# Half of the decay exponentials replaced by products on GpSimd, with the cosine's bias an immediate and the first transform of u in pairs of row tiles

## The chip, the cores and the metric

One core of a Trainium2 chip runs the kernel. The metric is the device time of one execution in microseconds (us). Engines are named as in the profile: PE is TensorE, PEld its weight load, ACT is ScalarE, DVE is VectorE, POOL is GpSimd, SP is SyncE (it issues most DMAs).

## The reference

The input is u, 2048 x 448 (L x D). Two branches read it and are mixed by a gate.

```python
# branch a: a diagonal state space model (N = 256 complex modes per channel), as a convolution
dt = exp(log_dt)
A = -exp(log_A_real) + 1j * A_imag
P = exp((A * dt[:, None])[:, :, None] * arange(L))        # D x N x L
K = 2 * einsum("dn,dnl->dl", C * dt[:, None], P).real     # D x L
a = irfft(rfft(u.T, 2 * L) * rfft(K, 2 * L))[:, :L].T + u * D_skip
# branch b: attention of 16 heads in 4 segments of 512, with a memory carried along
for s in range(4):
    p = softmax(q_s @ k_s.T * scale + mask)
    o_s = g * (phi(q_s) @ M) / (phi(q_s) @ z + 1e-6) + (1 - g) * (p @ v_s)
    M, z = M + phi(k_s).T @ v_s, z + phi(k_s).sum(l)      # phi(t) = t + 1 or exp(t)
b = o @ wo
gate = sigmoid((u * gate_w).sum(-1))
out = gate * a + (1 - gate) * b
```

## The kernel before

The first half, to about 448 us, makes the convolution kernel K and, between, the projections of the attention; the second half transforms K and u, multiplies, transforms back and does the attention. The change is in the first half.

**Parameters.** prepare_params (L178) works out the decay rate la = exp(log_A_real) dt, the angles and the coefficients, split into three bf16 parts each (parts, L227) and sent through DRAM (SD, SP) to be read as matmul weights (tiles lh). The tile cab holds a factor by which EX is multiplied.

**Decays, angles, products, sums.** A lag l is 64 b + r. The kernel sum over the 256 modes is done as products of X (coarse lags 64 b, tile EX times cosine or sine) with Y (fine lags r, tile EY times cosine or sine). first_half (L312) goes over 28 J of 16 channels each; n = 2 J + c are 56 steps of 8 channels, and four n make a group g, 0 to 13.

- decays(g), L422: for each of the group's two J three calls of decay (L339): two matmuls (ps_arg<-ce,lh, one for each row half) and one Exp of 128x1024: EY(J,0), EY(J,1), then EX(J), which POOL multiplies by cab (scale, L353, one TENSOR_TENSOR of 128x1024, L359). Six exponentials a group.
- turns(n), L361: eight matmuls give the angle in turns. trig(n), L376: ACT makes sine, abs, and the cosine as the sine of pi/2 less that (bias tile bhp); the result is the tile cs, of which there are two buffers.
- product(n), L386: four DVE instructions: X (L393), Y (L397, L398 and L399). sums(n), L401: 32 small matmuls ps_k<-Y,X.

Exp and Sin lie in different tables of ACT, so each group has two table loads. The order on each engine is that of the program's code, with decays of a group behind the product of the group before.

**Feed.** What PE, ACT and DVE do between these steps is doled out by the class Feed (L465). Its steps come from two generators: project (L678: for each of four segments s the transposes of xin, the products with the value weights (values), and 8 units, each 12 matmuls with a weight tile w of 448 KB loaded from WD; units go in pairs, and "pe" behind a pair holds the generator until the next call of exps), and transform_u (L513: 32 tiles of a first transform of u, ps_m<-ut,s1u, evicted to gs and stored to GU). spend(us) runs steps until their own nominal costs use up the budget; a step with a negative cost ends a spend. exps, called ahead of each Exp in decay, lets a held pair go on. The budget is PLACE (L460) at the six places of decays and 1.7 at each n, times RATES for the group. What is left at the end is run by feed.rest.

**Split weights.** In project, weights() splits wq and wk into a high part (ACT) and a rest (POOL, L721), in two tiles wsp of their own, and stores them to WD (queue of SP, L1394). The units load w (L733, two buffers) from WD. hi and lo of a unit go to QD or KD (L767).

A matmul is recorded under L1370 (helper mm), a transpose under L1373, most ACT instructions under L1335 (act and copy). The tile ps_m stands for PSUM buffers that all these steps share.

## Time and profile before

| | |
|---|---|
| median of 3 runs | 873.04 us (870.07 to 874.4) |
| span of the profiled execution | 866.7 us |
| first half / second half | 448.1 / 418.6 us |
| busy PE, DVE, ACT, POOL | 753.7, 596.9, 539.2, 173.1 us |
| one group of four n, mean of the last twelve | 27.5 us |

The span is that of one execution taken by the profiler; the runs were timed apart, and their median is 6.3 us above it. A line of the grouped view reads: line, engine, operation, output<-inputs by the program's names, shapes, count, then busy time in us and mean ns of one, then the idle time ahead and what ended it. In the timeline the first two numbers are start and duration in us. In the windows view each engine has its busy time and, in brackets, its instructions; the last three columns are the granted clock of PE, the DMA share and GB/s.

### The profile page before, as it was taken

To read this page: it belongs to the slowest core of one execution; us is meant where nothing else is said; L and a number is where in the kernel's file an instruction comes from. 1 tells how busy PE (TensorE), PEld (TensorE's weight loads), DVE (VectorE), ACT (ScalarE), POOL (GpSimd) and SP (SyncE) were. 2 spreads that over 40 slices of the span, in tenths; PEclk is the share of its full clock that TensorE was granted. 3 is DMA by queue.
4 is the path that set the end of the run, shared out by engine and by line. 5 is a ranking of instruction groups with operands and counts; after the bars stand their busy time and mean duration, and the time that the engine had idled before them with its cause. 6 is when DMAs were issued, how large, how long until landed. Compare 5 with 4: busy or idle time off the path is not lost.

```text
span 866.7 us, 18996 instructions
## 1 busy us (share of the span) xinstructions
PE 753.7 (87%) x7575; PEld 410.3 (47%) x7597; DVE 596.9 (69%) x1160; ACT 539.2 (62%) x638; POOL 173.1 (20%) x217
## 2 busy tenths in 40 slices
PE   1687988998879988799979799999997998888997
PEld 1364655765547644476534444444443443343443
DVE  7988778777787777877648656656664747664564
ACT  4876989798997999979842255544453434431220
POOL 5224111001110011101100111222313124222110
PEclk9998999998999999999979689999999999878799
DMA  9347753334633255323569948557465545654873
GB/s 242 91 110 247 227 185 104 96 111 154 205 124 96 96 169 194 122 92 132 178 218 347 317 133 264 178 193 249 139 222 189 193 162 168 216 187 164 221 231 100
DMA packets 88290, 153.11 MB, mean 177 GB/s; under 512 B 20626, under 2 KB 57162, under 8 KB 88154
## 3 DMA queue, kind: packets, MB, share of 16 engines
q1 hardware_dynamic: 79130, 140.83, 50.2%
q10 hardware_dynamic: 7424, 9.18, 3.1%
q0 software_dynamic: 1648, 1.89, 0.7%
q8 instruction: 60, 0.98, 0.5%
q14 instruction: 28, 0.23, 0.1%
HBM read 90.87 MB, written 60.63 MB: 175 GB/s over the span
## 4 chain that ended last, share of the span: by engine, by line
PE 52%; ACT 16%; DVE 13%; issue 7%; DMA 7%; POOL 2%; SPq 1%; ACTq 0%; DVEq 0%; POOLq 0%
PE ps_a L1370 18%; PE ps_m L1370 16%; PE ps_pv L1370 7%; ACT cs L1335 7%; PE ps_arg L1370 4%; DVE jk L992 3%; PE ps_k L1370 3%; PE ps_m L1373 2%; ACT L1335 2%; DVE Y L397 2%; DMA WD<-wsp 1%; ACT EX L1335 1%; DMA dn<-pvs 1%; DVE Y L398 1%; DMA ident<-in_c_id 1%
## 5 line engine op out<-in xcount | busy, mean ns | idle before, releaser
L1023 ACT ACTIVATE PT<-ps_a 128x1024 f32<-128x1024 f32 (+1 forms) x96 | 84.5, 881 | 122.9 <-PE ps_a L1370 115.9
L992 DVE CUSTOM_DVE_ANT_0 jk<-ps_a,mk 128x512 f32<-128x512 f32 (+3 forms) x256 | 124.9, 488 | 49.6 <-PE ps_a L1370 42.3
L359 POOL TENSOR_TENSOR EX<-EX,cab 128x1024 f32<-128x1024 f32 x28 | 54.0, 1928 | 309.3 <-ACT EX L1335 286.3
L1335 ACT ACTIVATE cs<-ps_arg 128x1024 f32<-128x1024 f32 x111 | 107.3, 1021 | 2.7 <-DVE Y L398 2.4
L1370 PE MATMUL ps_a<-qu,ku 32*128 32x512 f32 (+3 forms) x768 | 92.9, 364 | 1.3 <-DVE mx L992 0.6
L1370 PE MATMUL ps_m<-xh,w 112*128 112x512 f32 x256 | 92.9, 412 | 0.7 <-DVE lo L762 0.5
L393 DVE TENSOR_TENSOR X<-EX,cs 128x1024 f32<-128x1024 f32 x56 | 70.5, 1260 | 23.2 <-ACT cs L1335 21.5
L1034 POOL TENSOR_SCALAR_AFFINE_SELECT PT<-PT 128x256 f32<-128x256 f32 (+1 forms) x96 | 47.1, 493 | 178.9 <-ACT PT L1023 178.7
L1370 PE MATMUL ps_k<-Y,X 128*32 128x64 f32 x3584 | 64.1, 226 | 11.8 <-DVE Y L398 11.8
L1370 PEld LDWEIGHTS ps_k<-Y,X 128*32 128x32 f32 x3584 | 54.9, 113 | 38.0 <-DVE Y L398 19.9
L397 DVE TENSOR_TENSOR Y<-EY,cs 128x1024 f32<-128x1024 f32 x56 | 70.0, 1251 | 0.0
L1370 PEld LDWEIGHTS ps_a<-qu,ku 32*128 32x128 f32 x768 | 64.8, 201 | 10.1 <-issue 3.2
L1335 ACT ACTIVATE cs<-cs,bhp 128x1024 f32<-128x1024 f32 x56 | 64.5, 1151 | 1.8
L1370 PE MATMUL ps_a<-ku,qu 32*128 32x512 f32 (+3 forms) x256 | 47.2, 404 | 16.0 <-DVE mx L992 8.4
L399 DVE SCALAR_TENSOR_TENSOR Y<-EY,cs 128x512 f32<-128x512 f32 x56 | 39.4, 704 | 30.5 <-ACT cs L1335 29.7
L1335 ACT ACTIVATE EY<-ps_arg 128x1024 f32<-128x1024 f32 x52 | 53.1, 1030 | 11.1 <-PE ps_arg L1370 10.0
L1370 PEld LDWEIGHTS ps_m<-xh,w 112*128 112x128 f32 x256 | 48.0, 188 | 20.0 <-issue 7.6
L1370 PEld LDWEIGHTS ps_a<-ku,qu 32*128 32x128 f32 x256 | 23.1, 195 | 62.7 <-issue 28.6
L1370 PE MATMUL ps_m<-xl,w 112*128 112x512 f32 x128 | 50.3, 393 | 0.0
L1370 PE MATMUL ps_arg<-ct,lh 64*128 64x512 bf16 x224 | 43.1, 386 | 8.1 <-ACT cs L1335 5.0
L1370 PEld LDWEIGHTS <-lh 64*128 64x128 bf16 x392 | 22.1, 95 | 50.6 <-issue 37.8
L604 DVE TENSOR_TENSOR pr<-ps_a,ks 128x896 f32<-128x896 f32 x32 | 34.7, 1085 | 15.7 <-PE ps_a L1370 15.4
(214 smaller groups left out, 1408.7 us busy)
## 6 DMA issues: line engine op xcount, KB each, us to landing
w<-WD SPq DMA_DIRECT2D x32, 448.0 KB
qu<-QD SPq DMA_DIRECT2D x16, 512.0 KB
ku<-KD SPq DMA_DIRECT2D x16, 512.0 KB
GU<-gs SPq DMA_DIRECT2D x32, 224.0 KB
GK<-gs SPq DMA_DIRECT2D x8, 896.0 KB
gk<-GK SPq DMA_DIRECT2D x32, 224.0 KB
gu<-GU SPq DMA_DIRECT2D x32, 224.0 KB
BB<-bs ACTq DMA_DIRECT2D x16, 448.0 KB
```

The source lines that it names most:

```text
L359: nc.gpsimd.tensor_tensor(o, o, cab, ALU.mult)
L393: v.tensor_tensor(X, ex, t[:, :, 0], ALU.mult)
L397: v.tensor_tensor(Y[:, :, :, :32], lo, y[:, :, :, ::-1], ALU.mult)
L398: v.tensor_tensor(Y[:, 0, :, 32:], ey[:, :, 32:], y[:, 0], ALU.mult)
L399: v.scalar_tensor_tensor(Y[:, 1, :, 32:], ey[:, :, 32:], -1.0, y[:, 1], ALU.mult, ALU.mult)
L604: nc.vector.tensor_tensor(pr[c], pt, ks.pop(c), ALU.mult)
L992: v.tensor_tensor_reduce(junk[:, :n], pt[:, x, o : o + n], k.mk[:, SEG - n :], 1.0, -3e38, ALU.add, ALU.max, mx[:, 3 - t, h : h + 1],)
L1023: nc.scalar.activation(PT[:, 2 * hp : 2 * hp + 2, 512 * b : 512 * b + n], pt[:, :, :n], AF.Exp, scale=SCALE)
L1034: nc.gpsimd.affine_select(sl, sl, pat, ALU.is_ge, 0.0, base=0, channel_multiplier=-1)
L1335: x = op(*args, **kw)
L1370: tc.keep_in_program_order(nc.tensor.matmul(*args, **kw))
L1373: tc.keep_in_program_order(nc.tensor.transpose(*args))
```

## The change

1. decays(g) has three exponentials in place of six. One of 128x1024 (tile ER) covers half of the coarse lags of both J of the group; the other half of EX comes from it by a product with gb2 = exp(-1024 la). One for each J (EY) covers fine lags 0 to 31; lags 32 to 63 come by a product with ga = exp(-32 la), in tiles EH. All these products are POOL's, of 128x512: for each J one by cab, one by gb2 and two EH, so eight a group in place of two of 128x1024.
2. ga and gb2 are made in the prologue: eight transposes of la and four Exp of 128x448.
3. The cosine's bias is the number pi/2 in place of the tile bhp.
4. transform_u issues the matmuls of both row halves of a u tile next to each other, then both evictions.
5. wsp is taken from the tag "w", which has two buffers, together with the units' w.
6. PLACE has three entries (1.24, 0.9, 0.9), the budget at each n is 1.87 in place of 1.7, and a pair that is "light" takes one filling step in place of two at each of two places.

The core of the diff:

```diff
@@ prepare_params
-    for _ in parts(k.SD, la, nc.gpsimd.tensor_tensor, k.pdma):
+    for _ in parts(k.SD, la, nc.gpsimd.tensor_tensor, k.pdma, new("lr", early)):
         pass
+    for nt in range(2):
+        pt = k.ps("m")
+        for j in range(4):
+            k.tr(
+                pt[:, 112 * j : 112 * j + 112], la[:, j, 128 * nt : 128 * nt + 128], k.ident[:112, :112]
+            )
+        for t, steps in ((k.ga, 32.0), (k.gb2, 1024.0)):
+            nc.scalar.activation(by_j(t[:, nt]), by_p(pt), AF.Exp, scale=-steps)
@@ first_half
-    def decay(J, blk):
+    def exps(x, pt):
+        feed.exps()
+        act(x.rearrange("p c t x -> p t c x"), pt.rearrange("p t (c x) -> p t c x", c=2), AF.Exp, scale=-1.0)
+
+    def decay_x(J):
 
         pt = k.ps("arg")
-        for nt in range(2):
-            r, kw = rows(nt)
-            k.mm(pt[:, nt], lt[J][r, 2], k.ce[r, blk], start=True, stop=True, **kw)
-        if blk < 2:
-            out = EY[J, blk] = gy.tile([128, 2, 512], F32, tag="EY", name="EY", bufs=6)
-        else:
-            out = EX[J] = gy.tile([128, 2, 512], F32, tag="EX", name="EX", bufs=2)
-        feed.exps()
-        act(out, pt, AF.Exp, scale=-1.0)
-        if blk == 2 and J > 1:
-            scale(J)
+        for a in range(2):
+            for nt in range(2):
+                r, kw = rows(nt)
+                k.mm(
+                    pt[:, nt, 256 * a : 256 * a + 256], lt[J + a][r, 2], k.ce[r, 512:],
+                    start=True, stop=True, **kw,
+                )
+        raw = gy.tile([128, 2, 2, 256], F32, tag="ER", name="ER", bufs=1)
+        exps(raw, pt)
+        for a in range(2):
+            EX[J + a] = raw[:, a]
+            if J > 0:
+                scale(J + a)
 
     def scale(J):
-        o = EX[J]
-        if True:
-            cab = k.cab[:, :, 16 * J : 16 * J + 16].unsqueeze(3).broadcast_to([128, 2, 16, 32])
-            o = o.rearrange("p t (d c) -> p t d c", c=32)
-            nc.gpsimd.tensor_tensor(o, o, cab, ALU.mult)
+
+        r = EX[J].rearrange("p t (d c) -> p t d c", c=16)
+        EX[J] = gy.tile([128, 2, 512], F32, tag="EX", name="EX", bufs=2)
+        o = EX[J].rearrange("p t (d c) -> p t d c", c=32)
+        lo, hi = 16 * J, 16 * J + 16
+        nc.gpsimd.tensor_tensor(o[:, :, :, :16], r, over(k.cab, lo, hi, 16), ALU.mult)
+        nc.gpsimd.tensor_tensor(o[:, :, :, 16:], o[:, :, :, :16], over(k.gb2, lo, hi, 16), ALU.mult)
+
+    def decay_y(J):
+
+        pt = k.ps("arg")
+        for nt in range(2):
+            r, kw = rows(nt)
+            k.mm(pt[:, nt], lt[J][r, 2], k.ce[r, :512], start=True, stop=True, **kw)
+        EY[J] = gy.tile([128, 2, 2, 256], F32, tag="EY", name="EY", bufs=3)
+        exps(EY[J], pt)
+        for c in range(2):
+            EH[J, c] = gy.tile([128, 2, 256], F32, tag="EH", name="EH", bufs=4)
+            d = 16 * J + 8 * c
+            nc.gpsimd.tensor_tensor(
+                EH[J, c].rearrange("p t (d l) -> p t d l", l=32),
+                EY[J][:, c].rearrange("p t (d l) -> p t d l", l=32),
+                over(k.ga, d, d + 8, 32), ALU.mult,
+            )
@@ trig
-        act(fl, fl, AF.Sin, bias=k.bhp, scale=-TWO_PI)
+        act(fl, fl, AF.Sin, bias=math.pi / 2, scale=-TWO_PI)
@@ product
-        v.tensor_tensor(Y[:, 0, :, 32:], ey[:, :, 32:], y[:, 0], ALU.mult)
-        v.scalar_tensor_tensor(Y[:, 1, :, 32:], ey[:, :, 32:], -1.0, y[:, 1], ALU.mult, ALU.mult)
+        v.tensor_tensor(Y[:, 0, :, 32:], hi, y[:, 0], ALU.mult)
+        v.scalar_tensor_tensor(Y[:, 1, :, 32:], hi, -1.0, y[:, 1], ALU.mult, ALU.mult)
@@ decays
-        for J in (2 * g, 2 * g + 1):
-            for blk in range(3):
-                decay(J, blk)
-                if g > 0 and J % 2 and blk == 1:
-                    sums(4 * g - 1)
-                if g > 0:
-                    k.exps = 3 * (J % 2) + blk >= 2
-                    feed.spend(PLACE[3 * (J % 2) + blk] * RATES[g])
-                    k.exps = False
+        for i, (f, J) in enumerate(((decay_x, 2 * g), (decay_y, 2 * g), (decay_y, 2 * g + 1))):
+            f(J)
+            if g > 0 and i == 1:
+                sums(4 * g - 1)
+            if g > 0:
+                k.exps = i >= 1
+                feed.spend(PLACE[i] * RATES[g])
+                k.exps = False
...
-        feed.spend(1.7 * RATES[n // 4])
+        feed.spend(1.87 * RATES[n // 4])
...
-PLACE = (1.24, 0.62, 0.62, 0.62, 0.0, 0.62)
+PLACE = (1.24, 0.9, 0.9)
@@ transform_u
-        for h in range(2):
+    todo = [(w, h) for w in range(16) for h in range(2)]
+    while todo:
+        n = 2 if k.pairs and todo[0][1] == 0 else 1
+        now, todo = todo[:n], todo[n:]
+        pts = []
+        for w, h in now:
...
+            k.mm(pt[:, :D], k.s1u[r], uts[w][r], start=True, stop=True)
+            pts.append(pt)
+        for (w, h), pt in zip(now, pts):
             gs = up.tile([128, D], F32, tag="gs", name="gs", bufs=3)
             k.copy(gs, pt[:, :D], AF.Copy)
             nc.sync.dma_start(guv[h, :, w], gs)
-            yield 0.9
+        yield 0.9 if n == 1 else 1.2
@@ project
-    wsp = [pp.tile([112, 4, 2, 4, 32], F32R, name=f"wsp{i}") for i in range(2)]
+    wsp = [
+        pp.tile([112, 4, 2, 128], F32R, tag="w", name="wsp", bufs=2).rearrange("p g b (j e) -> p g b j e", e=32)
+        for i in range(2)
+    ]
...
-                    for _ in range(2 if light else 0):
+                    for _ in range(1 if light else 0):
                         yield -next(filling, 0.1)
```

In the changed kernel a matmul is under L1416, a transpose under L1419, ACT's instructions under L1380, the products of EX under L376 (cab) and L377 (gb2), EH under L390, a load of w under L778 and a store of WD under L1440.

SP's queue about the last stores of the split weights (WD<-wsp) and the first loads of w, before:

```order
L733 DMA w<-WD 112x1024 x2
L1394 DMA WD<-wsp_212 112x4x256
L328 DMA lh_91<-SP 48x2x128 x2
L1394 DMA WD<-wsp_213 112x4x256
L1394 DMA WD<-wsp_212 112x4x256
L322 DMA lh_92<-SD 48x128 x2
L1394 DMA WD<-wsp_213 112x4x256
L733 DMA w<-WD 112x1024
```

and the same place of the changed kernel:

```order
L1440 DMA WD<-wsp 112x4x256
L335 DMA lh_91<-SP 48x2x128 x2
L1440 DMA WD<-wsp 112x4x256 x2
L329 DMA lh_92<-SD 48x128 x2
L778 DMA w<-WD 112x1024
L1440 DMA WD<-wsp 112x4x256
L778 DMA w<-WD 112x1024
```

The first two loads of w stood ahead of the last four stores; now the first stands behind the last but one and the second behind the last.

PE at the end of the first half, from the sums of the last but one n to the first matmuls of transform_k (ps_a<-kb,s1k), before:

```order
L1370 MATMUL ps_k_5300<-Y_5364,X_5363 32x64 x32
L1370 MATMUL ps_m_5464<-ut_4381,s1u_189 128x448
L1370 MATMUL ps_m_5469<-ut_5405,s1u_189 128x448
L1370 MATMUL ps_m_5474<-ut_5405,s1u_189 128x448
L1370 MATMUL ps_m_5479<-ut_5424,s1u_189 128x448
L1370 MATMUL ps_k_5300<-Y_5414,X_5413 32x64 x32
L1370 MATMUL ps_m_5525<-ut_5424,s1u_189 128x448
L1370 MATMUL ps_a_5556<-kb_495,s1k_1925 128x448 x2
```

and in the changed kernel, where the rows left out are of the same kinds (values and units of segment 3, each 12 matmuls):

```order
L1416 MATMUL ps_k_5010<-Y_5057,X_5056 32x64 x32
L1416 MATMUL ps_k_5010<-Y_5099,X_5098 32x64 x32
L1419 MATMUL ps_m_5195<-ident_130,xin_5193 112x128 x4
L1419 MATMUL ps_m_5204<-ident_130,xin_5202 112x128 x4
L1419 MATMUL ps_m_5213<-ident_130,xin_5211 112x128 x4
L1419 MATMUL ps_m_5222<-ident_130,xin_5220 112x128 x4
...
L1416 MATMUL ps_m_5250<-wvh_201,xh_5191 128x450
...
L1416 MATMUL ps_m_5267<-xh_5191,w_5265 128x512
...
L1416 MATMUL ps_m_5517<-ph_5422,macc3_206 128x512
L1416 MATMUL ps_a_5557<-kb_505,s1k_2315 128x448 x2
```

Behind the last sums stood one u tile; now the whole of segment 3 of project stands there: 16 transposes of xin, 48 matmuls of values, 96 of the units and 13 others.

PE in group 1, between the last decay matmuls (ps_arg<-ce,lh) and the first turns (ps_arg<-ct,lh), of the changed kernel; xh and xl are the split inputs, w_826 is the first w that is loaded:

```order
L1416 MATMUL ps_arg_813<-ce_132,lh3_93 128x512
...
L1416 MATMUL ps_m_828<-xh_216,w_826 128x512
L1416 MATMUL ps_m_828<-xl_217,w_826 128x512
L1416 MATMUL ps_m_828<-xh_216,w_826 128x512 x2
...
L1416 MATMUL ps_arg_849<-ct_188,lh2_92 128x512
```

Before, two units (w_764 and w_779) stood between the decay matmuls and ahead of these turns; now one does, and its w_826 is loaded from behind the stores above.

66 lines of the change are left out of this document (34 added, 32 removed).

## The prediction

> **What bounds the kernel now.** The page's busy times come first.
>
> ```profile
> PE 753.7 (87%) x7575; PEld 410.3 (47%) x7597; DVE 596.9 (69%) x1160; ACT 539.2 (62%) x638; POOL 173.1 (20%) x217
> ```
>
> TensorE (PE) leads over the whole span, but the change touches only the first half, so I cut the span where its stages meet: at the table load that opens the exponentials of group 1 (76.4) and the one of group 2 (104.8), at the end of the last cosine (436.2), and at the first matmul of the kernel's transform (448.1).
>
> ```profile
> 76.40:104.80 28.40, 27.64 (x342) 17.81 (x347) 20.34 (x24) 22.74 (x25) 7.47 (x5) 1.00 0.80 240
> 104.80:436.20 331.40, 300.92 (x4440) 191.03 (x4432) 251.35 (x350) 298.41 (x341) 45.90 (x24) 0.97 0.42 138
> 436.20:448.10 11.90, 7.55 (x94) 3.45 (x83) 6.21 (x13) 3.63 (x8) 0.00 (x0) 0.73 0.51 175
> 200.50:227.50 27.00, 24.85 (x346) 15.05 (x346) 20.14 (x27) 24.64 (x29) 3.82 (x2) 0.87 0.48 155
> sum 330.30, PE 296.25 PEld 187.07 DVE 247.90 ACT 292.49 POOL 43.98; mean PE 24.69 PEld 15.59 DVE 20.66 ACT 24.37 POOL 3.67
> ```
>
> The columns are length, then busy time of PE, PEld, DVE, ACT, POOL. The fourth line is one group; the last sums twelve windows, one for each group of four n from 117.7 to 448 us. A group takes 27.5 us with 24.7 of PE and 24.4 of ACT (ScalarE): two engines near full at once, DVE (VectorE) at 20.7. The timeline of ACT and of DVE in one group shows how they interlock:
>
> ```profile
> 217.57 1.28 ACT L1335 ACT_TABLE_LOAD   x1
> 218.87 0.60 ACT L1335 ACTIVATE e<-ps_m 128x512 f32<-128x512 f32 x1
> ...
> 220.88 2.09 ACT L1335 ACTIVATE EY<-ps_arg 128x1024 f32<-128x1024 f32 x2
> 223.25 1.02 ACT L1335 ACTIVATE EX<-ps_arg 128x1024 f32<-128x1024 f32 x1 [0.28 <-PE ps_arg L1370]
> 224.17 1.94 ACT L1335 ACTIVATE EY<-ps_arg 128x1024 f32<-128x1024 f32 x2
> 226.43 1.02 ACT L1335 ACTIVATE EX<-ps_arg 128x1024 f32<-128x1024 f32 x1 [0.32 <-POOL EX L359]
> 227.47 1.28 ACT L1335 ACT_TABLE_LOAD   x1
> 228.76 1.94 ACT L1335 ACTIVATE cs<-ps_arg 128x1024 f32<-128x1024 f32 x2
> 230.74 1.15 ACT L1335 ACTIVATE cs<-cs,bhp 128x1024 f32<-128x1024 f32 x1
> ```
>
> ```profile
> 238.87 0.68 DVE L399 SCALAR_TENSOR_TENSOR Y<-EY,cs 128x512 f32<-128x512 f32 x1
> 239.47 1.22 DVE L393 TENSOR_TENSOR X<-EX,cs 128x1024 f32<-128x1024 f32 x1
> 240.60 1.22 DVE L397 TENSOR_TENSOR Y<-EY,cs 128x1024 f32<-128x1024 f32 x1
> 241.74 0.68 DVE L398 TENSOR_TENSOR Y<-EY,cs 128x512 f32<-128x512 f32 x1
> 242.34 0.68 DVE L399 SCALAR_TENSOR_TENSOR Y<-EY,cs 128x512 f32<-128x512 f32 x1
> ```
>
> The exponential phase (table load to table load, 217.57 to 227.47) takes 9.9 us; then four n of sine, abs and cosine. One n's four products take 242.34 - 238.87 = 3.47 us of DVE, back to back. The cs tile has two buffers, so ACT can't begin n+2 before DVE is done with n.
>
> **The change, stage by stage.** The profiled execution has a span of 866.7 us; the runs shown have a median of 873.04, 6.3 above it. I sum differences in the span and add them to the median.
>
> *Prologue and group 0 (to 76.4).* Three exponentials of 1.02 go. Four of half width, one table load (1.28) and eight transposes come, and POOL gets four EH products beside DVE's preparation. About 3 us against 3.6, and up to 4 more where POOL blocks DVE (below). Between -1 and +5; I take +2.5.
>
> *The cosine with an immediate.* Two sines in the prologue differ in this alone:
>
> ```profile
> L211 ACT ACTIVATE pin_c<-pin_g,bhp 112x1024 f32<-112x1024 f32 x1 | 1.1, 1148 | 0.0
> L211 ACT ACTIVATE pin_b<-pin_g 112x1024 f32<-112x1024 f32 x1 | 1.0, 1040 | 0.0
> ```
>
> So 0.11 us for each n, 0.4 a group. One n of ACT falls from 230.74 - 228.76 + 1.06 = 3.04 to about 2.95, counted in the period below.
>
> *Pairs of u tiles.* Matmuls on the two row halves now stand next to each other, as those of gk already do in the second half:
>
> ```profile
> L1370 PE MATMUL ps_m<-ut,s1u 64*128 64x448 f32 x64 | 31.2, 623 | 6.4 <-ACT gs L1335 4.3 <-DVE lo L764 1.5 <-DVE lo L762 0.5
> L1370 PE MATMUL ps_a<-gk,cf 64*128 64x448 f32 x128 | 34.8, 622 | 2.0 <-DVE pr L604 1.5
> ```
>
> With two records to a tile, 31.2/32 = 0.98 us of PE a tile against 34.8/64 = 0.54: 14 us over 32 tiles, one a group. But PE isn't the bound once ACT's work falls (24.7 less three pairs of decay matmuls, less this and less what moves to the end, beside a period of 23). What hides it is ACT and DVE; I count nothing, and -4 where groups heavy on PE gain.
>
> *The groups (104.8 to 436.2).* ACT loses three exponentials: 24.4 - 3.1 - 0.4 = 20.9 is its floor. POOL gets eight products of 128x512 (EX twice, by cab and by gb2, for two J, and four EH) for two of 128x1024, and every one must be done before the products that read it. Nearest rows:
>
> ```profile
> L359 POOL TENSOR_TENSOR EX<-EX,cab 128x1024 f32<-128x1024 f32 x28 | 54.0, 1928 | 309.3 <-ACT EX L1335 286.3
> L1121 POOL TENSOR_TENSOR xt<-xt,dbc 128x448 f32<-128x448 f32 x16 | 18.3, 1157 | 23.0 <-DMA xt<-in_A_u 19.6 <-issue 3.4
> ```
>
> Half of the first is 0.96; a line through both, 1.24 at 512 columns; the second scaled by columns, 1.32. I take p = 1.1. POOL and DVE also block each other; group 0 shows it in the timelines of both:
>
> ```profile
> 59.96 4.23 POOL L359 TENSOR_TENSOR EX<-EX,cab 128x1024 f32<-128x1024 f32 x2 [22.95 <-DVE cab L211]
> 62.76 2.50 DVE L393 TENSOR_TENSOR X<-EX,cs 128x1024 f32<-128x1024 f32 x1 [0.35 <-ACT cs L1335]
> 64.15 2.11 POOL L721 TENSOR_TENSOR wsp<-win,wsp 112x448 fp32r<-112x448 f32 x1
> 65.19 2.15 DVE L397 TENSOR_TENSOR Y<-EY,cs 128x1024 f32<-128x1024 f32 x1
> 70.53 1.21 DVE L397 TENSOR_TENSOR Y<-EY,cs 128x1024 f32<-128x1024 f32 x1
> ```
>
> A product of 1.21 alone takes 2.15 to 2.50 beside a POOL product: they run one after the other, so their times add. The Trainium skill ("SBUF — State Buffer", section "Who interferes with whom") says that a DVE instruction with two SBUF inputs and a GpSimd instruction that reads SBUF exclude each other, the later one fully blocked; these rows agree. By that section of the Trainium skill, all of POOL's new work beside products would be lost to DVE: 8 x 1.1 = 8.8 us a group at most, a period of 20.7 + 8.8 = 29.5 if none of it lay beside other work.
>
> The period follows from a chain. Count from the table load that opens the exponentials: 1.28, then e and hi of two units 2.0, then the joint half-lag exponential 1.0: POOL starts at 4.3. Two more exponentials and a table load bring the first sine to 7.7 to 8.7. POOL's order is four EX products, then four EH, and the group's first DVE product (L399's) reads EH: it can't begin before 4.3 + 5p = 9.8. From there DVE's products of the first n (3.5) and POOL's last three take turns, so that n is done at 4.3 + 8p + 3.5. Then the second n (3.5), which frees the cs that ACT needs for the fourth n (3.0). Period = 14.3 + 8p: 23.1 at p = 1.1, 22.0 at 0.96, 24.9 at 1.32. I add 0.5 for groups heavy in project steps (before, such groups took 28.8 to 30.1). The stage is 331.4/27.5 = 12.05 periods: 12.05 x 23.6 = 284, **-47** (-60 to -25).
>
> *Group 1.* The split weights (wsp) now share two buffers with the weights w of project, so the first w can't be loaded before wsp's last stores are done, and SP issues it behind them. From the chain of waits (a store of 5.0, a load of 5.5, 12 matmuls of a unit) and the timeline:
>
> ```profile
> 77.85 4.95 DMA WD<-wsp
> 80.81 0.59 PE L1370 MATMUL ps_m<-xh,w 112*128 112x512 f32 x1
> 85.60 5.53 DMA w<-WD
> 90.58 1.94 ACT L1335 ACTIVATE cs<-ps_arg 128x1024 f32<-128x1024 f32 x2
> 91.17 3.01 PE ps_m L1370 x12
> ```
>
> Before, the first unit ran at 80.81 and group 1's first sine at 90.58. Now the last splits are subtracted about 84 to 85, stored by 90, loaded by 95.5 (or some 3 earlier, if the release comes with the next to last store). In PE's order that unit's 12 matmuls (3.0) stand ahead of the turns that the first two sines read; they begin around 98 instead of 90.6: +7.5. Two units had run by then; now one has, and the other's 3.0 us fall into the sine phase, where PE had little to spare (27.6 busy of 28.4). **+10.5**; +4.5 with the early release, up to +14 if later loads of w don't keep up either.
>
> *The end (436.2 to 448.1).* Feed now gets seven spends a group in place of ten, three in place of six moments at which a held pair may go on, and steps with a negative cost still end a spend. In PE's order of the changed kernel the whole fourth segment of project is left behind the last sums and ahead of ps_a: 16 transposes of xin, 4 values (48 matmuls), 8 units (96), 13 others. Before, only u tiles stood there.
>
> ```profile
> 435.14 1.15 ACT L1335 ACTIVATE cs<-cs,bhp 128x1024 f32<-128x1024 f32 x1
> 448.13 1.13 PE L1370 MATMUL ps_a<-kb,s1k 32*128 32x448 f32 x4
> L1373 PE MATMUL ps_m<-ident,xin 128*112 128x128 f32 x64 | 14.3, 384 | 26.7 <-DMA xin<-in_A_u 13.5 <-ACT gs L1335 6.6 <-DVE xl L858 6.6
> ```
>
> Units: 8 x 3.0 = 24. Values: 4 x 3.0 x 450/512 = 10.5. Transposes 16 x 14.3/64 = 3.6. The 13 others at a unit's 3.0/12: 3.2. Sum 41.3. Two buffers of w and a load of 5.5: of the last six units every other waits 2.5, 5 in all, and the chain from xin over xh and xl into the values about 2. Behind the last cosine come three products (2.9) and the last sums (about 1.3). So 52.5 where 11.9 stood: **+40.5**. Bounds: no waits, +33; each load bare (4.3 per unit), +47.
>
> *The second half* is untouched: 0.
>
> Sum: 2.5 - 47 + 10.5 + 40.5 = +6.5 on 873: **879.5 us**.
>
> **The rivals.**
> 1. *Faster: POOL's products are short and hide.* If p is the half of 1928, the stage gives -60; if the blocking is only partial and the group falls to ACT's floor plus little (21.5), -72. With group 1 at +8 and the end at +36 the sum is -14 to -26: about 855. For it: POOL starts while DVE still evicts from PSUM, and no steady-state product of before lies beside POOL, so the overlap may cost less. PE and ACT both do less in total. Against it: PE's own work in the stage, 301 less 41 (moved to the end), 14 (u in pairs) and some 10 (decay matmuls), plus some 10 moved in, is 246, which would be 95% of 12.05 x 21.5. It decides at a period of (331.4 - 53.5)/12.05 = 23.1, where the stage gives back the 53.5 us that the other three terms cost; the forecast's 23.6 is not far from it.
> 2. *Slower by much: POOL blocks DVE for more.* Beyond the three EH products that I let take turns, EX of a new group meets the last n's products. With p = 1.24 and 0.5 more of blocking the period is 25.2, the stage -28, the sum +26: 899. It needs DVE to be still in products when POOL starts; in the timeline they end 2 to 4 us into the exponential phase, just where POOL begins. The Trainium skill's section above is the rule behind it, at its strictest.
> 3. *No gain in the groups, since PE stays the bound there* (the change doesn't do what it says): 27 us a period, stage -6, sum +47: 920. Against it: PE loses the fourth segment and three decay pairs a group.
> 4. *No difference:* the gain of the groups and the new end cancel, within 4 us of 873.
>
> **How the numbers follow.** The forecast, where it ends above +0.5%, has 0.38, rival 2 has 0.13, rival 3 0.02: slower 0.53. Rival 4 has 0.15. Rival 1 has 0.32; the term with the widest bounds is p, and its lower end crosses zero. 0.5% (4.4 us) is about what a measurement of this kernel tells from no change. The range takes the lower end of the groups with the middle of the rest (-60 is 13 below, the other terms low together take some 12 more: 855) and rival 2 above (902).
>
> **What would show it.** A table load every 23 to 24 us in the groups, with POOL busy 8 to 9.5 us in each; at 21 rival 1 holds, above 25 rival 2. The first product of a group waiting for POOL's EH, and products of 1.2 stretched to 2.3 beside POOL. The first unit's matmul at 92 to 96 waiting for DMA w<-WD. ACT's last cosine near 402, and then some 48 us of ps_m matmuls with ACT under a third busy before ps_a. I would be wrong if the segment at the end ran beside other work, or if p came out under 0.9.

## The result and the profile after

| | before | after |
|---|---|---|
| median of 4 runs each, us | 873.72 (870.07 to 875.47) | 906.93 (904.66 to 910.07) |
| profiled execution, its span | 866.7 | 904.3 |

The change makes the kernel slower: ratio 1.0416 (95% interval 1.0349 to 1.0483), above the range of the prediction. The direction was right, the size was not. Ratios, here and in the experiments, compare executions in the faster of a kernel's two states; medians are of all its executions. The profiled execution of the changed kernel took 906.73 us. Cut at the same places as before (table loads that open the exponentials of groups 1 and 2, end of the last cosine, first ps_a of the kernel's transform), the two spans differ so:

| stage | before | after | difference | predicted |
|---|---|---|---|---|
| prologue and group 0 | 76.4 | 82.9 | +6.5 | +2.5 |
| group 1 | 28.4 | 40.9 | +12.5 | +10.5 |
| groups 2 to 13 | 331.4 | 300.8 | -30.6 | -47 |
| end, last cosine to ps_a | 11.9 | 51.7 | +39.8 | +40.5 |
| second half | 418.6 | 428.0 | +9.4 | 0 |
| sum | | | +37.6 | +6.5 |

Two terms missed by much: the groups by 16.4 us, the second half by 9.4. The prologue missed by 4. The first line of the changed kernel's page and POOL's new groups (busy time, mean ns of one, idle before):

```profile
PE 761.0 (84%) x7549; PEld 418.0 (46%) x7549; DVE 609.0 (67%) x1151; ACT 501.5 (55%) x609; POOL 243.8 (27%) x301
L376 POOL TENSOR_TENSOR EX<-ER,cab 128x512 f32<-128x512 f32 x28 | 29.9, 1089 | 217.7 <-ACT ER L1380 206.6
L390 POOL TENSOR_TENSOR EH<-EY,ga 128x512 f32<-128x512 f32 x56 | 66.4, 1213 | 5.6 <-ACT EY L1389 4.9
```

The products take the 1.1 to 1.2 us that the prediction took, and ACT gave up 37.7 us (539.2 to 501.5). Neither is where it went wrong. The windows of the changed kernel, by stage (length, then busy time of PE, PEld, DVE, ACT, POOL, granted clock, DMA share, GB/s), the second and third rows being two single groups:

```profile
82.90:123.80 40.90, 32.51 (x427) 20.66 (x416) 22.82 (x27) 19.58 (x22) 11.98 (x11) 0.87 0.58 176
148.50:177.80 29.30, 24.81 (x371) 16.32 (x372) 25.69 (x36) 21.83 (x27) 8.49 (x8) 0.94 0.31 100
177.80:200.20 22.40, 18.83 (x322) 10.35 (x322) 13.13 (x15) 19.14 (x22) 8.57 (x8) 0.92 0.31 96
424.60:476.30 51.70, 45.05 (x310) 35.45 (x310) 21.32 (x38) 17.65 (x31) 2.12 (x2) 0.93 0.54 182
476.30:904.30 428.00, 382.69 (x2470) 173.55 (x2469) 254.11 (x688) 160.92 (x199) 88.87 (x152) 0.90 0.61 202
```

```profile
123.80:424.60 300.80, 256.33 (x4041) 158.83 (x4041) 242.23 (x307) 248.63 (x287) 106.06 (x96) 0.94 0.38 124
```

Over the twelve groups (mean 25.1) POOL's load is even, 8.5 us in the long group and 8.6 in the short, while the period swings from 22.4 to 29.3 with the work that Feed puts in: PE 24.8 against 18.8, DVE 25.7 against 13.1. PE's busy time in the stage fell by 44.6 us (300.92 to 256.33); almost as much, 37.5, came up in the end (7.55 to 45.05).

What DVE's products waited for in the groups (total, times, longest):

```profile
DVE Y L436 <- ACT cs L1380: 22.4, 11, 4.3
...
DVE Y L436 <- POOL EH L390: 1.5, 1, 1.5
```

The first product of a group hardly ever waits for POOL: once in twelve groups. The chain through POOL, on which the forecast's period rested, isn't there. In 11 of the 12 groups that product waits for ACT's cs. And ACT waits for PE's decay matmuls and turns (ps_arg), more than before. The two longest totals in the groups before, then after:

```profile
ACT EX L1335 <- PE ps_arg L1370: 8.5, 17, 1.2
ACT EY L1335 <- PE ps_arg L1370: 8.2, 15, 1.6
```

```profile
ACT EY L1380 <- PE ps_arg L1416: 19.1, 14, 2.8
ACT L1380 <- PE ps_arg L1416: 10.1, 4, 5.1
```

Group 1 is as foretold, and a little worse. From the chain of waits, then PE's first unit, after the change:

```profile
84.68 3.39 DMA WD<-wsp
...
88.68 1.13 POOL wsp L766
89.83 3.22 DMA WD<-wsp
...
93.12 3.61 DMA w<-WD
```

```profile
96.87 0.76 PE L1416 MATMUL ps_m<-xh,w 112*128 112x512 f32 x1 [7.05 <-DMA w<-WD]
```

The first w (93.12) is loaded when the last store but one has landed, and that store (89.83) waited for its split of the weights, which waited for the store before it. POOL's EX products stand behind that split and ahead of the last one only. The first unit starts at 96.87 where 92 to 96 was expected, in a group that itself starts 6.5 us later.

The end, from the chain of waits, shows units alternating with bare loads of w:

```profile
459.77 3.48 DMA w<-WD
...
463.38 3.02 PE ps_m L1416 x12
466.42 5.14 DMA w<-WD
...
471.69 3.85 PE ps_m L1416 x14
...
476.60 0.41 SPq L812
...
479.67 6.50 DMA ku<-KD
```

Its last rows lead into the second half: the last unit's results are stored to KD from SP's queue at 476.60 (L812), the loads of ku from KD stand behind, and ku's first load (6.50 us) lands at 486.2, with PE waiting for it. Before, KD's last store was issued at 431.7, 18 us ahead of the first load of ku. What PE waited for over the second half, after and then before:

```profile
PE ps_a L1416 <- DMA ku<-KD: 10.2, 2, 5.4
```

```profile
PE ps_a L1370 <- DMA ku<-KD: 4.5, 1, 4.5
```

The longer of the two waits (5.4, to 486.26) is new; the other (4.9, to 521.02) is the one that before has, too (4.5, to 483.52). Behind the new wait PE ran on a lower clock. The second and third 10 us of the second half, after and then before:

```profile
486.30:496.30 10.00, 8.89 (x48) 5.09 (x48) 6.58 (x19) 1.83 (x2) 0.00 (x0) 0.67 0.76 315
496.30:506.30 10.00, 8.96 (x42) 4.52 (x44) 5.44 (x19) 1.83 (x2) 0.00 (x0) 0.50 0.46 185
```

```profile
458.10:468.10 10.00, 8.82 (x62) 4.21 (x64) 8.88 (x31) 2.09 (x4) 0.00 (x0) 1.00 0.98 365
468.10:478.10 10.00, 9.65 (x64) 3.78 (x60) 8.13 (x20) 3.17 (x4) 0.61 (x1) 1.00 0.82 307
```

PE is nearly as busy, but in these 20 us it gets 90 matmuls done in place of 126, at a granted clock of 0.50 to 0.67 in place of 1.00. The end of the wait that both kernels have lies 35.4 us behind the start of the second half before (483.52 - 448.13) and 44.7 after (521.02 - 476.32): 9.3 of the 9.4 us are lost by then.

### The profile page after: what moved, and what is told of

It reads as the page before. It is cut to its first block, busy times and chain, and to the rows that moved or that the text cites. A ratio compares the mean times of both kernels' runs of the same rounds, so it can differ in the third digit from the quotient of the medians.

```text
span 904.3 us, 19003 instructions
## 1 busy us (share of the span) xinstructions
PE 761.0 (84%) x7549; PEld 418.0 (46%) x7549; DVE 609.0 (67%) x1151; ACT 501.5 (55%) x609; POOL 243.8 (27%) x301
## 4 chain that ended last, share of the span: by engine, by line
PE 52%; DVE 16%; ACT 14%; DMA 8%; issue 6%; SPq 2%; POOL 1%; ACTq 0%; DVEq 0%; POOLq 0%
PE ps_a L1416 19%; PE ps_m L1416 18%; PE ps_pv L1416 7%; ACT cs L1380 7%; PE ps_arg L1416 4%; PE ps_k L1416 3%; DVE jk L1037 3%; DVE Y L434 2%; DVE X L428 1%; ACT L1380 1%; PE ps_m L1419 1%; DMA ku<-KD 1%; DMA w<-WD 1%; DMA WD<-wsp 1%; DVE Y L435 1%
## 5 line engine op out<-in xcount | busy, mean ns | idle before, releaser
L1380 ACT ACTIVATE cs<-ps_arg 128x1024 f32<-128x1024 f32 x111 | 107.4, 1022 | 17.8 <-PE ps_arg L1416 15.7
L1416 PE MATMUL ps_m<-xh,w 112*128 112x512 f32 x256 | 91.6, 413 | 11.8 <-DMA w<-WD 10.3
L1416 PE MATMUL ps_k<-Y,X 128*32 128x64 f32 x3584 | 69.4, 235 | 32.7 <-DVE Y L435 31.0
L1416 PE MATMUL ps_a<-qu,ku 32*128 32x512 f32 (+3 forms) x768 | 92.8, 363 | 1.3 <-DVE mx L1037 0.6
L376 POOL TENSOR_TENSOR EX<-ER,cab 128x512 f32<-128x512 f32 x28 | 29.9, 1089 | 217.7 <-ACT ER L1380 206.6
L1416 PEld LDWEIGHTS ps_k<-Y,X 128*32 128x32 f32 x3584 | 59.0, 119 | 58.9 <-DVE Y L435 44.8
L434 DVE TENSOR_TENSOR Y<-EY,cs 128x1024 f32<-128x1024 f32 x56 | 72.5, 1294 | 0.0
L1416 PEld LDWEIGHTS ps_a<-qu,ku 32*128 32x128 f32 x768 | 64.6, 200 | 10.1 <-issue 3.2
L390 POOL TENSOR_TENSOR EH<-EY,ga 128x512 f32<-128x512 f32 x56 | 66.4, 1213 | 5.6 <-ACT EY L1389 4.9
L1416 PE MATMUL ps_a<-ku,qu 32*128 32x512 f32 (+3 forms) x256 | 48.6, 419 | 18.9 <-DMA ku<-KD 10.2
L1416 PEld LDWEIGHTS ps_m<-xh,w 112*128 112x128 f32 x256 | 49.0, 191 | 31.5 <-issue 15.7
L436 DVE SCALAR_TENSOR_TENSOR Y<-EH,cs 128x512 f32<-128x512 f32 x56 | 43.8, 783 | 28.0 <-ACT cs L1380 23.1
L1380 ACT ACTIVATE cs<-cs 128x1024 f32<-128x1024 f32 x56 | 59.3, 1059 | 1.8
L1416 PEld LDWEIGHTS ps_a<-ku,qu 32*128 32x128 f32 x256 | 23.7, 201 | 67.8 <-issue 34.3
L1416 PE MATMUL ps_arg<-ct,lh 64*128 64x512 bf16 x224 | 45.6, 409 | 7.7 <-ACT cs L1380 5.9
L1416 PE MATMUL ps_m<-xl,w 112*128 112x512 f32 x128 | 50.8, 397 | 0.0
L1416 PE MATMUL ps_m<-wo,pvs 128*128 128x448 f32 x96 | 42.6, 590 | 1.6 <-ACT tb L1172 1.4
```

The costliest lines, as they stand in the source:

```text
L376: nc.gpsimd.tensor_tensor(o[:, :, :, :16], r, over(k.cab, lo, hi, 16), ALU.mult)
L390: nc.gpsimd.tensor_tensor(EH[J, c].rearrange("p t (d l) -> p t d l", l=32), EY[J][:, c].rearrange("p t (d l) -> p t d l", l=32), over(k.ga ...
L434: v.tensor_tensor(Y[:, :, :, :32], lo, y[:, :, :, ::-1], ALU.mult)
L436: v.scalar_tensor_tensor(Y[:, 1, :, 32:], hi, -1.0, y[:, 1], ALU.mult, ALU.mult)
L1380: x = op(*args, **kw)
L1416: tc.keep_in_program_order(nc.tensor.matmul(*args, **kw))
```

## The experiments

Ratios are to the kernel before, run on the same chip, with 95% intervals; each altered kernel ran 4 to 12 times. What had to be told apart: does POOL set the period of the groups, or does PE, as rival 3 had it, so that the stage's -30.6 us is only work put off to the end?

### e1: Feed doesn't stop at breaks (after)

```diff
-        while self.due > 0 and not (self.held or self.done or self.ends and self.waiting):
+        while self.due > 0 and not (self.held or self.done):
```

> The changed kernel, with one line altered: a step of project with a negative cost no longer ends a spend, so segment 3 comes out of the feed inside the groups. Theory A (work left behind): the end falls from 51.7 us (last cosine to ps_a) to about 13, the second half loses the 9.4 us that it had gained, and the groups take up the moved work where PE still had room: PE was busy 256 of 300.8 us there and gets some 38 more, so the twelve groups grow from 301 to about 318. Together 906.9 - 39 - 9 + 18 = 877 us (868 to 886). Rival B (POOL and DVE bind the groups, so that nothing more fits in): the groups grow by all that the end loses, and the time stays at 898 or more.

Measured: 902.56, ratio 1.0333 (1.0255 to 1.0411). The end fell from 51.7 to 5.9 us and the second half from 428.0 to 412.2, but the prologue with group 0 grew by 21 (PE waited 17.9 us for one w that is now wanted ahead of its store), and the groups take 28.7 each:

```profile
130.91:475.26 344.35, 303.02 (x4314) 194.26 (x4309) 267.81 (x346) 262.46 (x309) 108.40 (x96) 0.93 0.40 130
```

PE's longest totals of waits from 60 to 500 us:

```profile
PE ps_m L1416 <- DMA w<-WD: 19.3, 3, 17.9
PE ps_m L1416 <- ACT pkT L1380: 17.8, 10, 3.0
PE ps_m L1419 <- ACT gs L1380: 10.1, 3, 3.4
```

All the work is back in the groups and the gain is gone; part of the loss is the experiment's own, since the breaks had let PE do other things while ACT answered (pkT, gs). The forecast of this run was missed, and the time is the one that its rival named: the groups grow by 43.5 us, nearly all that the end loses (45.8). So e1 by itself doesn't speak against POOL and DVE as the bound; e4 and e5 do.

### e2 and e8: the shared buffers of wsp, taken out and put in

e2 gives the changed kernel its two wsp tiles back (to make room, EY has two buffers and EH three); e8 gives the kernel before the shared ones and nothing else.

```diff
-    wsp = [
-        pp.tile([112, 4, 2, 128], F32R, tag="w", name="wsp", bufs=2).rearrange("p g b (j e) -> p g b j e", e=32)
-        for i in range(2)
-    ]
+    wsp = [pp.tile([112, 4, 2, 4, 32], F32R, name=f"wsp{i}") for i in range(2)]
```

> The changed kernel, with the split weights in two tiles of their own again, as before (for the room EY has 2 buffers in place of 3, EH 3 in place of 4). Theory A (the first load of w waits for the wsp stores): the first unit starts near 85 in place of 96.9 us, group 1 falls from 40.9 to about 30 us, the rest stays: 896 us (893 to 900). Rival B (group 1 waits for something else, such as POOL's products or PSUM): less than 3 us, 904 or more.

> The kernel before with the split weights in the buffers of w and nothing else changed. If the shared buffers cost what the first unit's wait shows, group 1 grows from 28.4 by 5 to 10 us: 880 us (877 to 883). If the wait in the changed kernel comes from POOL's products ahead of the splits, which this kernel has not, less than 3 us: under 875.

Measured: e2 893.37, ratio 1.0256 (1.0186 to 1.0326); e8 876.15, ratio 1.0107 (1.0061 to 1.0154). In e8, group 1 takes 10.2 us more than before (28.4 to 38.6), the groups 2.7 less, and the rest is unchanged; its window and PE's first unit:

```profile
76.55:115.11 38.56, 30.29 (x342) 19.34 (x347) 21.00 (x24) 22.78 (x25) 7.65 (x5) 0.87 0.58 172
```

```profile
89.09 0.76 PE L1373 MATMUL ps_m<-xh,w 112*128 112x512 f32 x1 [7.75 <-DMA w<-WD]
```

So the shared buffers alone are the +10.5 that the prediction gave group 1. But taking them out of the changed kernel brings group 1 only from 40.9 to 38.2, since later loads of w still stand behind stores that wait for POOL: the third is issued at 97.94, behind a store (95.84) whose split stood behind EX products. In e2 the second half took 420.3, 7.7 less than after, which nothing in its edit touches. So e2's time came out as forecast, but mostly not by the forecast's cause: group 1 was to fall to 30.

### e3: both edits (after)

> Both alterations together. Theory A (the two losses are separate and add): 906.9 - 30 - 11 = 866 us (857 to 876), below the kernel before. Rival B (they are one queue of work, so that the second mends what the first has mended already): 875 or more.

Measured: 886.68, ratio 1.014 (1.003 to 1.025): end 5.9, second half 415.6, groups 337.4. Nearer to before, and still nothing gained in the groups. The forecast of 866 was missed.

### e4: no EH products on POOL (after)

```diff
-            EH[J, c] = gy.tile([128, 2, 256], F32, tag="EH", name="EH", bufs=4)
-            d = 16 * J + 8 * c
-            nc.gpsimd.tensor_tensor(
-                EH[J, c].rearrange("p t (d l) -> p t d l", l=32),
-                EY[J][:, c].rearrange("p t (d l) -> p t d l", l=32),
-                over(k.ga, d, d + 8, 32), ALU.mult,
-            )
+            EH[J, c] = EY[J][:, c]
```

It leaves out the factor ga for fine lags 32 to 63, and with it half of POOL's products.

> The changed kernel without the EH products on POOL: DVE reads EY in their place, so the factor ga is left out of the fine lags 32 to 63. Theory A (the chain POOL to DVE to cs to ACT sets the period of the groups with little project work): these fall from 23.3 to about 21 us, where ACT's own work ends it, the heavy groups (28 to 29.6 us) stay, so 12 groups lose 12 to 24 us: 889 us (883 to 896). Rival B (the groups are set by PE and the feed): within 4 us of 906.9.

Measured: 900.99, ratio 1.0339 (1.0268 to 1.0409). The twelve groups in one window:

```profile
123.29:425.39 302.10, 262.36 (x4041) 163.19 (x4041) 233.93 (x307) 248.68 (x287) 50.83 (x48) 0.91 0.38 123
```

POOL's busy time halves and the stage is as long as in after (302.1 against 300.8), group by group within 1.6 us. So a chain through POOL's EH doesn't set the period. (The median is 5.9 us under after's, with intervals that overlap; the execution in the trace took 906.58 us, as after's did.) The four EX products of a group were not taken out; ACT waited for them once, 2.0 us, in the groups of after. The run also prices the blocking of DVE by the EH products: DVE's busy time for the same 307 instructions falls by 8.3 us (242.23 to 233.93), 0.7 a group, and the stage gains nothing by it.

### e5 and e6: budgets that bring the work back into the groups

e5 raises the budgets of the changed kernel; e6 is e5 with wsp tiles of their own, as in e2.

```diff
-        feed.spend(1.87 * RATES[n // 4])
+        feed.spend(2.05 * RATES[n // 4])
-RATES = (1.65, 1.65, 1.24, 1.55, 1.55, 1.17, 1.17, 1.48, 1.55, 1.17, 1.17, 1.48, 1.48, 1.65)
+RATES = (1.65, 1.95, 1.5, 1.75, 1.6, 1.25, 1.25, 1.6, 1.6, 1.25, 1.25, 1.55, 1.55, 1.75)
```

> The changed kernel with larger feed budgets (2.05 at each n, RATES raised by up to 0.26 in groups 1 to 12), the breaks behind steps of negative cost kept: segment 3 comes out inside the groups, but PE gets other work between a transpose and the copy that it waits for. Theory A (the loss is the work left behind, and the run without breaks lost by PE waiting for pkT and gs): PE waits for pkT stay under 5 us, the twelve groups take about 324 us (as 25.1 of PE a group took 27.6 before), the end 13, the second half about 420: 883 us (876 to 890). Theory B (the groups are bound so that moved work costs its full length wherever it stands): groups 340 or more, 899 us or more.

> The same with the split weights in tiles of their own (EY 2, EH 3 buffers). Own tiles took 13 us off the changed kernel, some 3 to 7 of it in group 1 and the rest in the second half's clock. Theory A: 6 to 10 us under the run with larger budgets alone, 875 us (866 to 884), about the kernel before. Theory B: 890 or more.

Measured: e5 878.57, ratio 1.0132 (1.0067 to 1.0197); e6 875.84, ratio 1.0063 (1.0023 to 1.0102). The windows of the groups and of the end in e5:

```profile
125.20:453.70 328.50, 299.49 (x4287) 192.08 (x4287) 259.22 (x347) 260.75 (x310) 103.51 (x96) 0.94 0.44 144
453.70:459.93 6.23, 1.94 (x65) 1.73 (x65) 4.64 (x10) 2.03 (x5) 1.68 (x2) 0.66 0.28 88
```

Both times are as forecast. The budgets alone take back 1.0416 - 1.0132 = 2.8% (some 25 us): the end shrinks by 45.5, the second half by 7.3, and the groups grow by 27.7. The work left behind costs much more alone at the end than among the groups. And with it back, the groups take 328.5 where the kernel before, with 37.7 us more of ACT's work, takes 331.4.

### e9 and e10: less work for PE, with three exponentials and with six

Both leave out 4 of the 12 matmuls of each unit and 8 of the 12 of each tile of values (products with the low parts); e9 does so in e6, e10 in the kernel before.

```diff
-            for a, b in ((0, 0), (0, 1), (1, 0)):
-                k.mm(pt, w[:, kt, a], x[b][:, kt], start=(n == 0), stop=(n == 11))
+            for a, b in ((0, 0), (1, 0)):
+                k.mm(pt, w[:, kt, a], x[b][:, kt], start=(n == 0), stop=(n == 7))
...
-                for a, b in ((xh, wvh), (xh, wvl), (xl, wvh)):
+                for a, b in ((xh, wvh),):
```

> The changed kernel with larger feed budgets and own tiles for the split weights, with PE work taken away: each unit of project leaves out the product of the weights' high part with the inputs' rest (4 of 12 matmuls), values leave out both products with a rest (8 of 12). That is about 31 + 26 us of PE, some 50 of it in the groups; ACT, DVE and POOL keep theirs. Theory C (once all of project is inside the groups, PE sets them, so that ACT's saved exponentials find nothing to shorten): the twelve groups fall from 333 to about 290 us, near ACT's 21.7 a group and its waits: 834 us (826 to 846). Theory D (round trips between the engines set the groups, no engine's sum): 333 to about 322, 862 us or more.

> The kernel before with the same matmuls left out. Theory C: ACT's 24.9 us a group becomes the bound at once; with its waits the groups fall only from 331 to about 315 us: 852 us (846 to 858), so the changed kernel's version is ahead by 12 to 20 us, which is what its exponentials are worth without PE in the way. Theory D: both fall by about the same, and the difference between the two versions stays that of the full ones (5 us the other way).

Measured: e9 846.41, ratio 0.9762 (0.9672 to 0.9851); e10 865.58, ratio 0.998 (0.9939 to 1.002). The windows of the groups in e6, e9 and e10, in this order:

```profile
117.07:449.90 332.83, 305.24 (x4287) 192.41 (x4287) 260.65 (x347) 260.89 (x310) 103.48 (x96) 0.92 0.43 143
```

```profile
116.37:421.30 304.93, 256.81 (x4086) 151.16 (x4086) 259.61 (x347) 259.06 (x310) 104.71 (x96) 0.95 0.47 155
```

```profile
106.30:437.40 331.10, 276.24 (x4230) 160.82 (x4218) 250.94 (x350) 296.33 (x341) 46.12 (x24) 0.92 0.42 137
```

| length of the groups (PE busy, ACT busy) | PE's full work | less for PE |
|---|---|---|
| six exponentials | 331.4 (301, 298) | 331.1 (276, 296) |
| three exponentials | 332.8 (305, 261) | 304.9 (257, 259) |

Taking matmuls from PE alone gives nothing, taking 37 us from ACT alone gives nothing, taking both gives 26. Either engine's work is enough to hold the stage at 331 us, and the change relieved one of them. The same table explains after: its groups have PE busy 256.3 and ACT 248.6 and take 300.8; e9's have 256.8 and 259.1 and take 304.9. The -30.6 of after needs PE's missing work, and that work came back at the end.

Three limits. The same matmuls are left out in both rows, but PE's busy time falls by 48 us in the lower and by 25 in the upper, where the granted clock is 0.92 in place of 0.97. The lower row has the larger budgets and the pairs of u tiles, too; e13 below is without them. And both forecasts were missed in size (290 us was expected for e9's groups, 315 for e10's): PE, ACT and DVE are each busy for 84 to 85% of e9's groups and 81 to 85% of after's, and what keeps them from being shorter was not found. DVE's sum alone isn't it in the full kernels: e9 has as much of it as e6 (259.6 and 260.7) and is 28 us shorter.

### e7, e11 and e12: the small parts alone, on the kernel before

e11 has the cosine's immediate alone:

```diff
-        act(fl, fl, AF.Sin, bias=k.bhp, scale=-TWO_PI)
+        act(fl, fl, AF.Sin, bias=math.pi / 2, scale=-TWO_PI)
```

e12 has the pairs of u tiles with the change to "light" pairs, as in the diff of the change; e7 has e11's edit, the same change to "light" pairs, and u tiles always in pairs.

> The kernel before with only the small edits: the cosine's bias an immediate, u in pairs of row tiles (1.2 of nominal cost a pair), one filling step in place of two in light pairs; six exponentials and the old feed. Theory A (both edits take work from the two full engines, 5 us from ACT and up to 14 from PE): 866 us (861 to 870). Theory B (round trips between engines set the groups, not their sums): within 3 us of 872.

> The kernel before with the cosine's bias an immediate and nothing else. It takes 56 x 0.09 = 5 us from ACT. If the groups are set by PE (theory C), within 2 us of the kernel before; if ACT shares in the bound, 866 us.

> The kernel before with u in pairs of row tiles exactly as in the change (1.2 of nominal cost a pair in the project's own steps, single tiles where the feed is held), and one filling step in place of two in light pairs. The run with both small edits was 18 us slower than before; the groups behind a long exponential phase waited for PE. Theory E (the pairs, by their lower nominal cost, let the budgets pull other steps forward into groups that are full): 885 us, and PE's time for the u matmuls stays at 31 to 33 us, so nothing is saved on PE. Theory F (the cosine's edit or the way that the pairs stood in that run was the cause): within 4 us of 870.

Measured: e7 887.74, ratio 1.0222 (1.0171 to 1.0274); e11 865.16, ratio 0.9972 (0.9934 to 1.001); e12 879.17, ratio 1.0161 (1.0058 to 1.0264). The cosine's edit gains 2.5 us by the medians, with an interval that holds zero. The pairs with the change to "light" cost 11.6 us by the medians (0.6 to 2.6%). Both theories of e7's forecast were missed, and e12 came nearer to theory E: PE's time for the u matmuls didn't fall (31.2 us before, 34.5 in e12). The window of the groups in e12, and one pair on PE:

```profile
105.98:457.84 351.86, 317.04 (x4386) 196.00 (x4374) 254.29 (x352) 299.66 (x342) 45.93 (x24) 0.94 0.41 133
```

```profile
213.79 1.02 PE L1377 MATMUL ps_m<-ut,s1u 64*128 64x448 f32 x2
216.09 1.02 PE L1377 MATMUL ps_m<-ut,s1u 64*128 64x448 f32 x2 [1.28 <-DVE tm L813]
```

The groups take 20 us more and the end and the second half 10 less. In the pair shown the second tile stands 1.28 us behind the first, until DVE has read another ps_m buffer (into tm), and PE's queue stands with it. That such gaps make up all of it was not shown: the granted clock is lower too (0.94 against 0.97).

### e13, e14 and e15: three exponentials with the old order of Feed

e13 is the changed kernel with single u tiles, two steps for "light", wsp tiles of their own (EY and EH with the fewer buffers of e2), and a second moment to spend behind each product, so that each group gets about as many steps as before the change. e15 is e13 with the shared wsp (and EY's and EH's buffers) again. e14 is e13 with less of the budget at the decays and more behind.

```diff
-        feed.spend(1.87 * RATES[n // 4])
+        feed.spend((1.0 if n >= 4 else 1.7) * RATES[n // 4])
         product(n)
+        if n >= 4:
+            feed.spend(0.95 * RATES[n // 4])
```

```diff
-PLACE = (1.24, 0.9, 0.9)
+PLACE = (0.8, 0.6, 0.6)
```

(The second is e14's, which has 1.1 at both moments of an n besides.)

> The changed kernel with everything but the decays and the cosine put back: u in single tiles, two filling steps in light pairs, split weights in own tiles (EY 2, EH 3 buffers), and the old RATES with a second spend at each n from group 1 on, so that every group gets the same steps of project and transform_u as in the kernel before. What is left is the three exponentials with POOL's products. Theory C (PE and ACT were both near full, so that the exponentials alone move the bound to PE): the groups gain only what PE saves on the decay matmuls, some 10 of 331 us, group 1 loses 5 to 7 through POOL's products ahead of the splits: 866 us (861 to 872). Theory G (with the old distribution of work ACT's 36 us come through): 850 us or less.

> The same, with less of the budget in the exponential phase (PLACE 0.8, 0.6, 0.6) and more at each n (1.1 and 1.1), since the phase is 3 exponentials shorter now and ACT waited there for PE (the second EY and the table load behind ps_arg). The steps of each group are the same. Theory H (ACT's waits in the exponential phase are PE's project work in front of the decay matmuls): 3 to 8 us under the run beside it, 860 us (855 to 866). Theory C alone (PE's sum, wherever the work stands): within 2 us of it.

> As the first of these, but with the split weights in the buffers of w as in the change (EY 3, EH 4 buffers). The kernel before took 7 to 10 us more with them. If the costs add: 8 to 10 us over the first, 875 us (870 to 881); if POOL's products ahead of the splits already make the wait, 3 us or less.

Measured: e13 871.98, ratio 1.0038 (0.9999 to 1.0078); e14 881.51, ratio 1.0153 (1.0105 to 1.0201); e15 879.11, ratio 1.0145 (1.0099 to 1.0191). e14 is judged by its time alone. Group 1 and the groups, in e13 and then in e15:

```profile
81.67:111.92 30.25, 28.28 (x357) 17.60 (x353) 21.80 (x23) 19.59 (x21) 13.29 (x11) 0.89 0.70 210
111.92:441.58 329.66, 293.50 (x4312) 187.72 (x4300) 265.53 (x347) 261.70 (x310) 107.09 (x96) 0.96 0.44 144
```

```profile
83.71:120.01 36.30, 28.98 (x341) 18.14 (x329) 19.35 (x23) 19.47 (x21) 12.00 (x11) 0.86 0.57 178
120.01:446.62 326.61, 291.99 (x4312) 188.45 (x4300) 264.25 (x347) 261.45 (x310) 106.79 (x96) 0.97 0.44 145
```

With buffers for wsp and work in each group about as before, three exponentials in place of six leave the kernel as long as before: groups 329.7 against 331.4. So it isn't the pairs or the budgets that hide the gain in e6. The shared buffers then cost 6 us in group 1, 7 in the median. Moving the work later (e14) makes it worse by 9.5; the idea behind that run, and its forecast of 860, fell. No version with three exponentials and all of the work beat the kernel before.

## Why the prediction was wrong

**Prologue: +6.5 for +2.5.** It ended beyond its upper bound of +5. Not followed further.

**Cosine: right.** L1380's mean is 1059 ns, 1151 before: 0.09 us each for the 0.11 taken, and e11 can't tell it from nothing.

**Pairs of u tiles: the saving on PE failed.** The forecast took 14 us off PE, read from gk's group, though it counted none of it in the time. The tiles' matmuls had 31.2 us of PE before and 32.8 after. On PE, in the changed kernel:

```profile
145.23 1.82 PE L1416 MATMUL ps_m<-ut,s1u 64*128 64x448 f32 x4
232.48 0.91 PE L1416 MATMUL ps_m<-ut,s1u 64*128 64x448 f32 x2
236.39 1.39 PE L1416 MATMUL ps_m<-ut,s1u 64*128 64x448 f32 x2 [0.48 <-ACT gs L1380]
381.87 1.02 PE L1416 MATMUL ps_m<-ut,s1u 64*128 64x448 f32 x4
```

Two row halves side by side take 1.02 for both tiles, as at 381.87, in one place only. Many of the tiles still go one by one, in the steps that fill (232.48 and 236.39); other pairs run one after the other (145.23). Alone, the pairs cost time (e12).

**Groups: -47 became -30.6; this is the step that failed.** The forecast let a chain through POOL set the period ("The period follows from a chain") and put PE aside ("PE isn't the bound once ACT's work falls"). The first half was wrong: "it can't begin before 4.3 + 5p" held in the order of the code, but DVE waited for EH once, 1.5 us, and in e4 half of POOL's products go without a change in the groups' length. p was right (1.09 to 1.21 us for 1.1) and didn't matter. The second half is what cost the gain: ACT's relief was given its full effect, and ACT came to wait for PE instead. With all of PE's work in the groups, 37 us less of ACT changed them by less than 3 us (e5, e6, e13: 328.5, 332.8, 329.7 for 331.4); only with PE's work reduced as well did they fall, to 304.9 (e9). PE's sum was too low besides: rival 1 put it at 246 us, with 14 saved by the pairs, and 256.3 were measured, with nothing saved by them.

**Group 1: right.** +12.5 for +10.5; e8 gives 10.2 for the shared buffers alone, with the mechanism that was named. In the changed kernel they aren't the only cause: with own buffers group 1 still takes 38.2 (e2), and only with the order of Feed changed as well does it fall to 30.3 (e13).

**End: right.** +39.8 for +40.5. What the sum missed is that this term and the gain of the groups are one thing: e5 puts the work back and both go, 45.5 from the end, 27.7 to the groups.

**Second half: 0 became +9.4.** "Untouched" held for its code. Stores to KD, AM and DM at the very end of the first half (476.2 to 478.6 on SP's queue) put ku's first load behind them, PE waited 5.4 us for it, and behind that wait the clock was at 0.50 to 0.67. The three traces with a long end (after, e2, e4) have such a wait of 5.3 to 5.9 us some 10 us into the second half, and none of the others has one. How the 9.4 us divide between wait and clock stays open, and so does the size: second halves of 412.2 to 423.7 stand in runs with a short end, 420.3 to 428.0 in those with a long one, and the two overlap.

**Rivals.** Rival 2 foresaw a period of 25.2 us and a stage of -28, and 25.1 and -30.6 came. That was luck: its cause, POOL's blocking of DVE for more, isn't there. The four products of an n took 219.1 us of DVE before and 227.7 after, all 56 n together, and e4 takes 8.3 us of DVE's time out of the stage without making it shorter. Rival 3, given 0.02, came nearest to the mechanism, with its 27 us a group: once all the work is in the groups they take 27.4 to 27.7 (e5, e6, e13). As it stands it was not right, since PE did lose the fourth segment and the groups fell; but that was a loan, paid back at the end. And PE alone isn't the bound either (e10). Rivals 1 and 2 both argued over POOL. The Trainium skill ("SBUF — State Buffer", section "Who interferes with whom") has a DVE instruction with two SBUF inputs contend with a GpSimd instruction that reads SBUF; the trace agrees, and shows how little of it there was. In the changed kernel a product of DVE beside POOL's EH, and the same product alone:

```profile
186.83 1.08 DVE L436 SCALAR_TENSOR_TENSOR Y<-EH,cs 128x512 f32<-128x512 f32 x1 [4.33 <-ACT cs L1380]
...
191.64 0.68 DVE L436 SCALAR_TENSOR_TENSOR Y<-EH,cs 128x512 f32<-128x512 f32 x1
```

That is 0.40 us more for the one instruction, and 8.3 for the whole stage by e4, where the prediction's strictest case had 8.8 for each group.

Left open: which of e13's waits stand in the place of the exponentials saved (11.7 us of ACT's there are for POOL's EX products), what holds after's groups at 300.8 us with no engine busy for more than 85% of them, why e2's second half is 7.7 us shorter than after's, and how much of e12's loss is the clock.

## What to carry to other kernels

Where two engines are each near 90% busy in a stage and wait for each other, work taken off one may give nothing, as here, so try a kernel with less work on the other engine too before the gain is counted. When a stage gets shorter, count first what work it lost: here the gain was gone when the work that had been put off to the end was put back. Buffers shared between the last stores of one thing and the first loads of the next cost a round trip (10.2 us in group 1 of e8), and a stage whose code is untouched can still pay for stores that end up just ahead of its loads.

## What the hardware showed

- After PE's wait of 5.4 us at the start of the second half, the granted clock stayed at 0.50 over 10 us in which PE was 90% busy (496.3 to 506.3), before it was back at 0.99. It had fallen in the wait (1.00 from 480 to 482 us, 0.50 from 484 to 486) and come back for a moment behind it (1.00 from 490 to 492). The kernel before has such a stretch, too, later and behind its own wait of 4.5 us for ku, with PE 95 to 99% busy:

```profile
488.10:498.10 10.00, 9.46 (x58) 6.17 (x57) 5.31 (x23) 3.59 (x5) 2.43 (x5) 0.50 0.83 278
498.10:508.10 10.00, 9.86 (x58) 3.80 (x58) 3.26 (x12) 4.14 (x6) 1.45 (x3) 0.57 0.38 129
```

  The Trainium skill ("TensorE: Matmul & The Clock Gate", section "Part 1: The HAM clock gate (the "warmup" mystery)") has the gate close after an idle window and open again after some 3.4 us of sustained work; the closing agrees with the rows, the quick opening doesn't. In group 1 of the changed kernel it does, nearly: behind the wait of 7.05 us the clock was 0.50 from 94 to 100 us and 1.00 from 102, with PE at work from 96.87. Those matmuls are of 112 rows, the ones of the slow stretch from 496.3 of 32 (ps_a<-kb,s1k 32*128). But 32-row ones ran at 1.00 in the kernel before, from 458.1 to 468.1 us, so the rows aren't the whole reason, and what is wasn't tried.
- One product of 128x512 on POOL took 1.09 us (L376) to 1.21 (L390) in the mean, 56% to 63% of the 1928 ns of one of 128x1024. L390's median is 1.05, so some of its products took much longer, up to 2.03.
